# GpSimd adds a constant to VectorE's magnitudes in place of shift matmuls

## The chip, the cores and the metric

The kernel runs on one core of a Trainium2 chip. The metric is device time in microseconds (us) for one launch. All engines of the core are in use: TensorE for matmuls (PE, with PEld for the weight loads that it overlaps), VectorE (DVE), ScalarE (ACT), GpSimd (POOL), and SyncE (SP), which issues all DMAs.

## The reference

Attention over a few inducing points, followed by a rational feed-forward layer. All data are float32.

```python
B, N, m, C = 4, 12480, 32, 128          # x: (4, 12480, 128), inducing: (32, 128)
def mab(q, kv):
    s = (q @ kv.transpose(0, 2, 1)) / sqrt(C)
    a = exp(s - s.max(-1, keepdims=True));  a /= a.sum(-1, keepdims=True) + 1e-9
    return a @ kv
h = mab(I, x)                           # 32 pooled rows per batch
x = mab(x, h).reshape(49920, 128)       # attention of every token to the 32 rows

h = x @ w_in                            # (49920, 2048)
P = a[0] + a[1]*h + a[2]*h**2 + a[3]*h**3
Q = 1 + |b[0]|*|h| + |b[1]|*h**2
out = (P / (Q + 1e-6)) @ w_out          # (49920, 128)
```

The kernel rewrites P/Q. After h is scaled, Q is a constant times (1 + |h|)^2 + c, and P/Q is a linear part, which needs no quotient, plus ((|h| + k1)(h + k2) + k3) times a factor proportional to 1/Q. The constants k1, k2 and k3 come from a and b.

## The kernel before

Work is cut into **units** of 480 tokens by 256 hidden columns. Eight units make a **block**, which is 480 finished output columns; there are 26 blocks per batch and 104 blocks, so 832 units. The attention weights and the pooled rows are folded into TensorE's operands: `st` holds the pooled rows times w_in, `at` the softmax weights, and a unit's h is `at` times `st`.

`fast_ticks` (L787) writes the program one **tick** per unit, even and odd units in turn, as an order that the scheduler keeps on each engine (`keep_in_program_order`). A tick takes a step of several units, which are at different ages. The steps, with a letter each, as they are spoken of from here on:

- **first** (L734): two matmuls of 480 columns, `hp<-at,st`. They write h to a PSUM room `hp`; there are three rooms of two banks.
- **M**, even units: VectorE takes the magnitude, `u<-hp`, by masking the sign bit, and writes half of a pair tile `u`. Odd units get |h| from ScalarE's Abs (`u<-hp,all`) into the other half. For odd units the constant k2 already stands in `st`, and Abs takes it off again with its bias.
- **S**, even units only (`add_shift`, L749): two matmuls `hp<-ones_rows,k_rows` add k2 to h in PSUM, once M has read it.
- **N** (`numerator`, L837): VectorE's `l<-u,all,hp`, (|h| + k1) times (h + k2), into one of twelve rooms `l`. When N has read h, its `hp` room is free.
- ScalarE runs Ln and, four ticks later, Sigmoid on the whole pair (`u<-u` and `u<-u,all`); u then holds the factor proportional to 1/Q. Four pairs get Ln in a row, then four Sigmoid, with a table load at each switch.
- **K**, even units, eleven ticks after M: VectorE's `l<-l,all,u`, (l + k3) times u.
- **T** and **X**, odd units (`last_on_pool`, L842): GpSimd's `u<-l,all` adds k3, writing over the even unit's u, which K must have read; then `l<-u` multiplies.
- **second** (L754), twelve ticks after first: TensorE multiplies the unit with w_out, `po<-l,w_out`, four passes, and so frees its `l` room. The eighth unit of a block adds the linear part (`po<-at,st`); then VectorE copies the block (`oT<-po`) and a DMA writes it out.

Between these steps `side` (L685) places the attention's own work, piece by piece, from two generators: `ahead` (scores and pooled rows of the next batch, its weights) and `attend` (softmax of tokens to the pooled rows). A piece is put into a tick when its estimated cost fits what the tick has to spare on VectorE, GpSimd or TensorE. ScalarE's copies of this work (`hl<-pa`, `eT<-pt`, `gt<-pgt`) are queued by `act` (L220) and written in the next tick by `run_act` (L227). Blocks of x come in by SyncE's queue: `x_rows` and the columns of kind a from six rooms `xa`, five ahead, the columns of kind b from five rooms `xTb`, four ahead. `spread` (L622) copies the weights from `hl` into the operand layout `at` with eight DMAs at a time.

Of the kernel before, what the change touches and what calls it, by code (L numbers as in the profile page):

```python
# [9 lines left out]
F32 = mybir.dt.float32  # L10
# [34 lines left out]
class Params:  # L45
# [46 lines left out]
    def derive(self):  # L92
# [28 lines left out]
        self.n += 2  # L121
        self.k2_parts = self.all[:, self.n - 2:self.n]
        part = self.pool.tile([P, 1], F32R, name="k2_part")
        self.nc.vector.tensor_copy(out=part, in_=self.k2)
        self.nc.vector.tensor_copy(out=self.k2_parts[:, 0:1], in_=part.bitcast(F32))
        self.nc.vector.tensor_tensor(out=self.k2_parts[:, 1:2], in0=self.k2, in1=part.bitcast(F32), op=sub)
# [52 lines left out]
class Kernel:  # L179
# [40 lines left out]
    def act(self, do):  # L220

        if self.direct:
            do()
        else:
            self.act_q.append(do)

    def run_act(self, exps=True):  # L227
        for do in self.act_q:
            do()
        self.act_q = []  # L230
        if exps:
# [35 lines left out]
    def weights(self):  # L267

        parts = []
        for f0 in range(0, self.F, BT):  # L270
            c = slice(f0, min(f0 + BT, self.F))
            parts.append((self.w_in_d[:, c], self.w_in[:, c], c.stop - c.start))
        for f0 in range(0, self.NF, 3):
            c = slice(f0, min(f0 + 3, self.NF))
            dst = self.w_out[:, c].rearrange("p f d -> p (f d)")
            parts.append((self.w_out_d[P * c.start:P * c.stop, :].rearrange("(f p) d -> p f d", p=P), dst, C * (c.stop - c.start)))
        for n, (src, dst, width) in enumerate(parts):
            tag, bufs = ("l", 12) if width > 2 * P else ("oT", 2)
# [58 lines left out]
    def pass1(self, b):  # L337
# [21 lines left out]
        self.xs[b] = [self.x_rows(b, n) for n in range(5)]  # L359
# [46 lines left out]
    def pooled(self, b, own=None):  # L406
# [6 lines left out]
        def turned(g):  # L413
# [7 lines left out]
            self.act(lambda: nc.scalar.activation(eT[:, :, rows], pt[0:TP, :, rows], AF.Identity, bias=0.0, scale=1.0))  # L421
# [8 lines left out]
        for g in range(self.NG):  # L430
# [4 lines left out]
            yield "wait", 0  # L435
            self.free()
            yield from self.landed("x", b, g)
            for k in range(HB * nb):
# [4 lines left out]
                if c == 0 and 4 * g + j + 5 < self.NB:  # L443
                    xs.append(self.x_rows(b, 4 * g + j + 5))
# [70 lines left out]
    def linear(self, b):  # L515
# [8 lines left out]
        self.act(lambda: nc.scalar.activation(gt, pt[:, 0:self.NF], AF.Identity, bias=self.params.lin_shift, scale=self.params.lin_scale))  # L524
        yield "wait", 0
# [70 lines left out]
    def quotients(self, b, r, nb, a):  # L596
# [10 lines left out]
        while self.spreads >= 2:  # L607
# [7 lines left out]
        self.act(lambda: nc.scalar.activation(hl[rows, 0], pt[rows, 0:BT], AF.Identity, bias=0.0, scale=1.0))  # L615
        yield "wait", 0
# [5 lines left out]
    def spread(self, b, r, nb, hl):  # L622
# [12 lines left out]
        self.spreads -= 1  # L635
        yield 0, 0, 0
# [150 lines left out]
    def fast_ticks(self, units):  # L787
# [4 lines left out]
        V, A, p = self.nc.vector, self.nc.scalar, self.params  # L792
# [3 lines left out]
        for t in range(n + 13):  # L796
            u, last, d = at(t), at(t - 1), at(t - 11)
            group, turn = divmod(t - 6, 8)
            w = at(8 * group + 2 * (turn % 4))
            if t % 2:  # L800
                if last:
                    self.add_shift(last)
                if at(t + 1):
                    self.first(at(t + 1))
# [3 lines left out]
                if at(t - 12):  # L808
                    self.second(at(t - 12))
# [3 lines left out]
                self.numerator(last)  # L813
            else:
                early = at(t - 12) and at(t - 12).key[2] > 0
                if early:
                    self.second(at(t - 12))
                else:
                    self.fetched = self.fetch()
                if at(t + 1):  # L820
                    self.first(at(t + 1))
# [15 lines left out]
    def numerator(self, u):  # L837
        if u:
            u.g = self.new(u, "l", 12)
            self.nc.vector.scalar_tensor_tensor(out=u.g, in0=u.u, scalar=self.params.k1, in1=u.h, op0=ALU.add, op1=ALU.mult)  # L840
# [32 lines left out]
    def before(self):  # L873
# [17 lines left out]
        col = self.cp.tile([P, 1], F32, name="k2_col")  # L891
        nc.vector.tensor_tensor(out=self.params.k2_parts, in0=self.params.k2_parts, in1=self.ident[:, 0:2], op=ALU.mult)
        nc.vector.tensor_reduce(out=col, in_=self.params.k2_parts, axis=mybir.AxisListType.X, op=ALU.add)
        self.ones_rows = self.cp.tile([2, BT], F32R, name="ones_rows")
        ones = self.cp.tile([2, 1], F32, name="one")
        nc.vector.memset(ones, 1.0)
        nc.vector.tensor_copy(out=self.ones_rows, in_=ones.broadcast_to((2, BT)))
        self.k2_rows = self.cp.tile([2, P], F32R, name="k2_rows")
        nc.vector.tensor_scalar(out=self.k2_rows, in0=ones.broadcast_to((2, P)), scalar1=col[0:2], scalar2=None, op0=ALU.mult)
# [5 lines left out]
    def main(self, fast):  # L905
# [6 lines left out]
        self.splits, self.spreads, self.scored, self.fetched = 0, 0, -1, False  # L912
# [60 lines left out]
```

## Time and profile before

| | us |
|---|---|
| median of 3 runs (lowest to highest) | 2725.65 (2723.05 to 2727.47) |
| profiled execution, its own time | 2723.84 |
| its span | 2722.0 |

| engine | busy us | share of the span |
|---|---|---|
| PE | 2522.6 | 93% |
| ACT | 2258.3 | 83% |
| DVE | 2133.3 | 78% |
| POOL | 1442.2 | 53% |

The profile's names for tiles are those of the code without numbers. `x832` is a count of instructions. In the chain of waits each step is followed back to what released it, so its sum is the span. A window's answer gives each engine's busy time between two moments. The moment at which a block's output DMA is issued serves as the border of blocks: the first is at 157.56 us, the last at 2717.50.

### The profile page before, as it was taken

What the parts mean: (1) busy time and instruction counts of PE and PEld (TensorE: products, weight loads), DVE (VectorE), ACT (ScalarE), POOL (GpSimd) and SP (SyncE); (2) the same over time, 40 slices, a digit from 0 to 9 for tenths busy, and PEclk for the clock granted to TensorE, in tenths of its full rate; (3) what the DMA queues carried; (4) which work ended last, traced back from release to release, by engine and by line L of the source; (5) the groups of instructions that cost most, each with busy time, mean ns of one, the idle gap of its engine ahead of it and who ended that gap; (6) DMA issues with size and microseconds to landing.
All of it is one profiled execution on the core that took longest, in us unless ns stands there. A gap on an engine that the chain in (4) does not pass through costs nothing.

```text
span 2722.0 us, 25250 instructions
## 1 busy us (share of the span) xinstructions
PE 2522.6 (93%) x8340; PEld 1343.6 (49%) x8340; DVE 2133.3 (78%) x2326; ACT 2258.3 (83%) x1591; POOL 1442.2 (53%) x1004
## 2 busy tenths in 40 slices
PE   7899989999998899999989999998999999899998
PEld 5545445555454455554545555444545445444443
DVE  6478877787878777877887778888888888888886
ACT  1478888888878987878898788898898988899996
POOL 2144555455545555555554555565555555655556
PEclk9699999999999999999999999999999999999999
DMA  9222112112221112022202210001101000000000
GB/s 255 76 76 77 37 33 58 51 55 66 76 58 44 30 39 73 19 76 87 64 16 73 62 29 28 21 18 55 48 26 41 29 22 22 26 19 26 19 19 16
DMA packets 117365, 133.77 MB, mean 49 GB/s; under 512 B 13544, under 2 KB 115816, under 8 KB 117224
## 3 DMA queue, kind: packets, MB, share of 16 engines
q1 hardware_dynamic: 117224, 132.06, 17.1%
q8 instruction: 68, 1.11, 0.2%
q14 instruction: 73, 0.60, 0.1%
HBM read 80.89 MB, written 25.56 MB: 39 GB/s over the span
## 4 chain that ended last, share of the span: by engine, by line
PE 63%; DVE 21%; ACT 7%; issue 3%; SPq 2%; DMA 2%; POOL 1%; DVEq 0%; ACTq 0%; POOLq 0%
PE po L163 32%; PE hp L163 20%; DVE l L163 11%; DVE u L163 9%; ACT u L163 5%; PE pd L163 3%; PE ph L163 3%; SPq L163 2%; PE pc L163 2%; ACT L163 1%; POOL l L163 1%; DMA raw<-w_in 1%; PE pl L163 1%; DVE oT L163 1%; PE pgt L163 1%
## 5 line engine op out<-in xcount | busy, mean ns | idle before, releaser
L163 PE MATMUL po<-l,w_out 128*128 128x480 f32 x3328 | 1482.0, 579 | 18.7 <-DVE oT L163 14.4
L163 DVE SCALAR_TENSOR_TENSOR l<-u,all,hp 128x960 f32<-128x960 f32 x832 | 1006.5, 1210 | 377.0 <-PE po L163 211.0
L163 POOL TENSOR_SCALAR u<-l,all 128x960 f32<-128x960 f32 x416 | 444.5, 1069 | 1105.1 <-DVE l L163 894.4
L163 POOL TENSOR_TENSOR l<-u 128x960 f32<-128x960 f32 x416 | 930.1, 2236 | 34.7
L163 PEld LDWEIGHTS po<-l,w_out 128*128 128x128 f32 x3328 | 627.1, 192 | 555.3 <-issue 447.2
L163 ACT ACTIVATE u<-u,all 128x1920 f32<-128x1920 f32 x416 | 776.0, 1889 | 1.2
L163 ACT ACTIVATE u<-u 128x1920 f32<-128x1920 f32 x416 | 737.3, 1797 | 1.1
L163 PE MATMUL hp<-at,st 128*128 128x480 f32 x1664 | 672.0, 485 | 33.6 <-DVE l L163 31.8
L163 ACT ACTIVATE u<-hp,all 128x960 f32<-128x960 f32 x416 | 438.1, 1053 | 288.8 <-PE hp L163 281.3
L163 DVE SCALAR_TENSOR_TENSOR l<-l,all,u 128x960 f32<-128x960 f32 x416 | 511.6, 1230 | 90.8 <-ACT u L163 90.6
L163 DVE TENSOR_SCALAR u<-hp 128x960 int32<-128x960 int32 x416 | 478.7, 1151 | 3.1 <-PE hp L163 3.1
L163 PEld LDWEIGHTS hp<-at,st 128*128 128x128 f32 x1664 | 280.8, 191 | 340.7 <-issue 270.9
L163 PE MATMUL hp<-ones_rows,k_rows 2*128 2x480 f32 x832 | 293.3, 431 | 114.1 <-DVE u L163 112.9
L163 ACT ACT_TABLE_LOAD x235 | 301.5, 1283 | 4.8 <-PEq L966 0.7
L163 PEld LDWEIGHTS hp<-ones_rows,k_rows 2*128 2x128 f32 x832 | 123.0, 185 | 309.1 <-DVE u L163 258.0
L163 DVE COPY oT<-po 128x480 f32<-128x480 f32 x104 | 68.2, 656 | 70.8 <-PE po L163 70.7
L163 PEld LDWEIGHTS pd<-HT,xTb 128*120 128x120 f32 x832 | 103.3, 198 | 13.8 <-issue 10.0
L163 PE MATMUL ph<-x,eT 120*32 120x129 f32 x832 | 104.9, 277 | 3.8 <-DMA x<-x_t 2.6
L163 PEld LDWEIGHTS ph<-x,eT 120*32 120x32 f32 x832 | 87.3, 111 | 31.6 <-issue 18.1
L163 PE MATMUL pd<-HT,xTb 128*120 128x32 f32 x832 | 99.7, 276 | 0.8 <-DVE hl L163 0.4
L163 PE MATMUL po<-at,st 128*128 128x480 f32 x104 | 79.6, 765 | 0.0
L163 PE MATMUL pc<-xTa,ind 128*128 128x480 f32 x156 | 69.9, 566 | 0.0
(92 smaller groups left out, 586.1 us busy)
## 6 DMA issues: line engine op xcount, KB each, us to landing
x<-x_t SPq DMA_DIRECT2D x104, 240.0 KB, 3.7
xTb<-x_c SPq DMA_DIRECT2D x104, 240.0 KB, 2.9
at<-hl SPq DMA_DIRECT2D x416, 60.0 KB, 2.0
out<-oT SPq DMA_DIRECT2D x104, 240.0 KB, 2.0
xTa<-x_c SPq DMA_DIRECT2D x78, 240.0 KB, 3.0
xTw<-x_c SPq DMA_DIRECT2D x5, 960.0 KB, 11.7
raw<-w_in SPq DMA_DIRECT2D x4, 480.0 KB, 15.0
raw<-w_out SPq DMA_DIRECT2D x5, 384.0 KB, 6.1
```

The source lines that it names most:

```text
L163: ins = call(*args, **kw)
```

## The change

1. S is gone, with the two-row operands `ones_rows` and `k2_rows` and the instructions that prepare them. In its place GpSimd adds k1 to M's result in the even tick, `l<-u,all` (**G**, a TENSOR_SCALAR of 128 x 960), and the even unit's N becomes (h + k2) times that: its tensor inputs are h in PSUM and l in SBUF, and it no longer reads u. The odd unit's N is as it was.
2. In an even tick M comes ahead of the odd unit's N on VectorE, and TensorE has first in another place of the tick.
3. There are fourteen rooms `l` in place of twelve. The even unit takes its room a tick earlier, at G.
4. ScalarE's queued copies are written one tick later than before, and the generator that queued one waits until it is written. The transposes `pa` also wait until two ticks have passed since the spread before the last was done.
5. `xa` has four rooms in place of six, `xTb` four in place of five; rows and columns of x are fetched three or four blocks ahead.

```diff
     def act(self, do):
+        done = []
         if self.direct:
             do()
         else:
-            self.act_q.append(do)
+            self.act_q.append((self.tick, do, done))
+            while not done:
+                yield "wait", 0
     def run_act(self, exps=True):
-        for do in self.act_q:
+        while self.act_q and self.act_q[0][0] < self.tick:
+            _, do, done = self.act_q.pop(0)
             do()
-        self.act_q = []
+            done.append(1)
...
     def x_rows(self, b, n):
-        t = self.ap.tile([TP, HB, C + 1], F32, tag="xa", name=f"x{b}_{n}", bufs=6)
+        t = self.ap.tile([TP, HB, C + 1], F32, tag="xa", name=f"x{b}_{n}", bufs=4)
...
-            t = self.ap.tile([C, BT], F32, tag="xTb", name=f"xTb{b}_{n}", bufs=5)
+            t = self.ap.tile([C, BT], F32, tag="xTb", name=f"xTb{b}_{n}", bufs=4)
...
-                if c == 0 and 4 * g + j + 5 < self.NB:
-                    xs.append(self.x_rows(b, 4 * g + j + 5))
+                if c == 0 and 0 < 4 * g + j < self.NB - 3:
+                    xs.append(self.x_rows(b, 4 * g + j + 3))
...
-        while self.spreads >= 2:
+        while self.spreads >= 2 or self.tick < self.sent[0] + 2 and not self.boot:
             yield "wait", 0
...
-    def add_shift(self, u):
-        for k in range(2):
-            self.nc.tensor.matmul(u.h[:, k], self.k2_rows, self.ones_rows, start=False, stop=True, skip_group_check=True)
...
+            late = at(t - 12) and at(t - 12).key[2] == 0
+            if late:
+                self.fetched = self.fetch()
+            if t % 2 and at(t + 1):
+                self.first(at(t + 1))
+            if at(t - 12) and not late:
+                self.second(at(t - 12))
+            if t % 2 == 0 and at(t + 1):
+                self.first(at(t + 1))
             if t % 2:
-                if last:
-                    self.add_shift(last)
-                if at(t + 1):
-                    self.first(at(t + 1))
                 if u:
                     u.u = last.pair[:, 1]
                     A.activation(u.u, u.h, AF.Abs, bias=p.back, scale=1.0)
-                if at(t - 12):
-                    self.second(at(t - 12))
                 if d:
                     V.scalar_tensor_tensor(out=d.g, in0=d.g, scalar=p.k3, in1=d.u, op0=ALU.add, op1=ALU.mult)
                     self.last_on_pool(at(t - 10), d)
-                self.numerator(last)
+                if last:
+                    V.scalar_tensor_tensor(out=last.g, in0=last.h, scalar=p.k2, in1=last.g, op0=ALU.add, op1=ALU.mult)
             else:
-                ...
-                self.numerator(last)
                 if u:
                     u.pair = self.mp.tile([P, 2, 2, BT], F32, tag="u", name=f"u{u.i}", bufs=7)
                     u.u = u.pair[:, 0]
                     V.tensor_scalar(out=u.u.bitcast(I32), in0=u.h.bitcast(I32), scalar1=0x7FFFFFFF, scalar2=None, op0=ALU.bitwise_and)
+                if last:
+                    last.g = self.new(last, "l", 14)
+                    V.scalar_tensor_tensor(out=last.g, in0=last.u, scalar=p.k1, in1=last.h, op0=ALU.add, op1=ALU.mult)
+                if u:
+                    u.g = self.new(u, "l", 14)
+                    G.tensor_scalar(out=u.g, in0=u.u, scalar1=1.0, scalar2=p.k1, op0=ALU.mult, op1=ALU.add)
...
-            if t % 2 == 0 and not early and at(t - 12):
+            if late:
                 self.second(at(t - 12))
```

How this moves the instructions is seen best in the last batch, where little attention work stands between the units. The names are batch, block and unit of the block (hp3_20_4 is unit 4 of block 20 of batch 3) and a running number. First TensorE around that unit, before:

```order
L163 MATMUL hp3_20_3_13539<-at3_5_0_13244,st_3_8873 128x480 x2
L163 MATMUL hp3_20_2_13525<-ones_rows_548,k2_rows_552 128x480 x2
L163 MATMUL hp3_20_4_13549<-at3_5_0_13244,st_3_8873 128x480 x2
L163 MATMUL po3_18_0_13472<-l3_18_7_13408,w_out_90 128x480 x2
L163 MATMUL po3_18_0_13472<-at3_4_1_13025,st_3_8873 128x480
```

and in the change:

```order
L157 MATMUL hp3_20_3_13133<-at3_5_0_12849,st_3_9162 128x480 x2
L157 MATMUL hp3_20_4_13143<-at3_5_0_12849,st_3_9162 128x480 x2
L157 MATMUL po3_18_0_13071<-l3_18_7_13009,w_out_90 128x480 x2
L157 MATMUL po3_18_0_13071<-at3_4_1_12638,st_3_9162 128x480
L157 MATMUL hp3_20_5_13158<-at3_5_0_12849,st_3_9162 128x480 x2
```

The shift of unit 2 is gone from between the firsts of units 3 and 4, which now stand back to back. VectorE over the same ticks, before:

```order
L163 SCALAR_TENSOR_TENSOR l3_20_3_13568<-u3_20_2_13544,all_196,hp3_20_3_13539 128x960
L163 TENSOR_SCALAR u3_20_4_13570<-hp3_20_4_13549 128x960
L163 SCALAR_TENSOR_TENSOR l3_19_2_13449<-l3_19_2_13449,all_196,u3_19_2_13434 128x960
L163 SCALAR_TENSOR_TENSOR l3_20_4_13587<-u3_20_4_13570,all_196,hp3_20_4_13549 128x960
L163 SCALAR_TENSOR_TENSOR l3_20_5_13595<-u3_20_4_13570,all_196,hp3_20_5_13565 128x960
```

and in the change:

```order
L157 TENSOR_SCALAR u3_20_4_13161<-hp3_20_4_13143 128x960
L157 SCALAR_TENSOR_TENSOR l3_20_3_13163<-u3_20_2_13136,all_193,hp3_20_3_13133 128x960
L157 SCALAR_TENSOR_TENSOR l3_19_2_13034<-l3_19_2_13034,all_193,u3_19_2_13030 128x960
L157 SCALAR_TENSOR_TENSOR l3_20_4_13165<-hp3_20_4_13143,all_193,l3_20_4_13165 128x960
L157 TENSOR_SCALAR u3_20_6_13187<-hp3_20_6_13171 128x960
```

The order was N, M, K, N and is M, N, K, N; the second N of a pair (unit 4) reads h and l where it read u and h. GpSimd, before:

```order
L163 TENSOR_SCALAR u3_19_0_13410<-l3_19_1_13432,all_196 128x960
L163 TENSOR_TENSOR l3_19_1_13432<-u3_19_0_13410 128x960
L163 TENSOR_SCALAR u3_19_2_13434<-l3_19_3_13467,all_196 128x960
L163 TENSOR_TENSOR l3_19_3_13467<-u3_19_2_13434 128x960
L163 TENSOR_SCALAR u3_19_4_13469<-l3_19_5_13494,all_196 128x960
```

and in the change:

```order
L157 TENSOR_SCALAR u3_19_0_13007<-l3_19_1_13032,all_193 128x960
L157 TENSOR_TENSOR l3_19_1_13032<-u3_19_0_13007 128x960
L157 TENSOR_SCALAR l3_20_4_13165<-u3_20_4_13161,all_193 128x960
L157 TENSOR_SCALAR u3_19_2_13030<-l3_19_3_13066,all_193 128x960
L157 TENSOR_TENSOR l3_19_3_13066<-u3_19_2_13030 128x960
```

G of unit 4 of block 20 stands between X of block 19's unit 1 and T of its unit 3. T of unit 3 waits for K of block 19's unit 2, whose u it writes over.

More of the change, by code (lines that the diff above doesn't have):

```diff
@@ L120, in derive @@
         self.back = self.ts(self.k2, -1.0, mult)
[L121 to L126, printed above, removed]
         top = self.mul(self.mul(self.mul(a3, alpha), self.mul(alpha, alpha)), self.recip(gamma))
@@ L277, in weights @@
         for n, (src, dst, width) in enumerate(parts):
-            tag, bufs = ("l", 12) if width > 2 * P else ("oT", 2)
+            tag, bufs = ("l", 14) if width > 2 * P else ("oT", 2)
             raw = self.mp.tile([P, width], mybir.dt.int64, tag=tag, name=f"raw{n}", bufs=bufs)
@@ L306, in columns @@
     def columns(self, b, kind):
-        depth = 5 if kind == "a" else 4
-        ts = [self.x_columns(b, n, kind) for n in range(depth)]
+        ts = [self.x_columns(b, n, kind) for n in range(4)]
         def turns():
             for n in range(self.NB):
-                if n + depth < self.NB:
-                    ts.append(self.x_columns(b, n + depth, kind))
                 yield ts.pop(0)
+                if n + 4 < self.NB:
+                    ts.append(self.x_columns(b, n + 4, kind))
         return turns()
@@ L358, in pass1 @@
             self.free()
-        self.xs[b] = [self.x_rows(b, n) for n in range(5)]
+        self.xs[b] = [self.x_rows(b, n) for n in range(4)]
         yield "v", 0.1
@@ L420, in turned @@
             eT = ap.tile([TP, HB, P], F32, tag="eT", name=f"eT{b}_{g}", bufs=2)
-            self.act(lambda: nc.scalar.activation(eT[:, :, rows], pt[0:TP, :, rows], AF.Identity, bias=0.0, scale=1.0))
+            yield from self.act(lambda: nc.scalar.activation(eT[:, :, rows], pt[0:TP, :, rows], AF.Identity, bias=0.0, scale=1.0))
             eTs.append(eT)
@@ L523, in linear @@
         gt = ap.tile([P, 512], F32, tag="gs", name=f"gt{b}", bufs=2)[:, 0:self.NF * M].rearrange("p (f m) -> p f m", m=M)
-        self.act(lambda: nc.scalar.activation(gt, pt[:, 0:self.NF], AF.Identity, bias=self.params.lin_shift, scale=self.params.lin_scale))
-        yield "wait", 0
+        yield from self.act(lambda: nc.scalar.activation(gt, pt[:, 0:self.NF], AF.Identity, bias=self.params.lin_shift, scale=self.params.lin_scale))
         self.free()
@@ L614, in quotients @@
         hl = ap.tile([P, 2, BT], F32R, tag="hl", name=f"hl{b}_{r}", bufs=2)
-        self.act(lambda: nc.scalar.activation(hl[rows, 0], pt[rows, 0:BT], AF.Identity, bias=0.0, scale=1.0))
-        yield "wait", 0
+        yield from self.act(lambda: nc.scalar.activation(hl[rows, 0], pt[rows, 0:BT], AF.Identity, bias=0.0, scale=1.0))
         yield "v", 0.65
@@ L635, in spread @@
         self.spreads -= 1
+        self.sent = self.sent[1], self.tick
         yield 0, 0, 0
@@ L812, in fast_ticks @@
                     self.last_on_pool(at(t - 10), d)
-                self.numerator(last)
-            else:
[L815 to L821, printed above, removed]
-                self.numerator(last)
+                if last:
+                    V.scalar_tensor_tensor(out=last.g, in0=last.h, scalar=p.k2, in1=last.g, op0=ALU.add, op1=ALU.mult)
+            else:
                 if u:
@@ L832, in fast_ticks @@
             self.side(u or units[-1])
-            if t % 2 == 0 and not early and at(t - 12):
+            if late:
                 self.second(at(t - 12))
         self.fetch()
[L837 to L840, printed above, removed]
     def last_on_pool(self, d, before):
@@ L852, in general_ticks @@
             self.first(u)
-            d, y, g, h = self.new(u, "u", 7), self.new(u, "l", 12), self.new(u, "l", 12), u.h
+            d, y, g, h = self.new(u, "u", 7), self.new(u, "l", 14), self.new(u, "l", 14), u.h
             r = self.ps_h.tile([P, 2, 512], F32, tag="hp", name=f"r{u.i}")[:, :, 0:BT]
@@ L890, in before @@
         self.params.derive()
[L891 to L899, printed above, removed]
         self.ceps = self.cp.tile([P, 1], F32, name="ceps")
```

7 lines of the change are left out of this document (3 added, 4 removed).

## The prediction

> **What bounds the kernel now.** I first cut the span into stretches with the windows view, at the moments where output blocks are issued, and counted the copies `oT<-po` in each. The columns are length, then busy time and count of PE, PEld, DVE, ACT and POOL.
>
> ```profile
> 157.56:1746.13 1588.57, 1507.67 (x5200) 815.95 (x5199) 1247.87 (x1321) 1339.09 (x945) 845.78 (x603) 0.99 0.19 53
> 1746.13:2678.96 932.83, 852.53 (x2524) 430.80 (x2524) 772.21 (x728) 841.47 (x579) 535.31 (x329) 0.99 0.10 28
> 2678.96:2722.00 43.04, 32.00 (x74) 13.87 (x74) 20.29 (x16) 21.34 (x14) 25.70 (x15) 0.96 0.06 20
> 2522.41:2544.76 22.35, 20.44 (x57) 10.04 (x57) 18.77 (x18) 20.72 (x15) 13.19 (x9) 1.00 0.03 11
> ...
> 157.56:1746.13 1588.57, 39.98 (x61) 0.99 0.19 53
> 1746.13:2678.96 932.83, 26.27 (x40) 0.99 0.10 28
> ```
>
> Stage A (the first row, 61 blocks) has the attention work of the next batch beside the units. It takes 1588.57 / 61 = 26.04 us a block; per block PE is busy 24.72, ACT 21.95, DVE 20.46, POOL 13.87. Stage B (40 blocks) has only the softmax of its own tokens: 23.32 a block, PE 21.31, ACT 21.04, DVE 19.31, POOL 13.38. The fourth row is one clean block of stage B: 22.35. There no engine is full, not even ACT with 20.72, so a chain must set the time. The chain of waits shows it, one pair of units after the other:
>
> ```profile
> 2544.66 1.20 DVE l L163
> 2545.86 1.08 DVE u L163
> 2546.94 0.04 issue
> 2546.98 1.33 PE hp L163 x4
> 2548.32 1.62 PE po L163 x4
> ...
> 2550.06 1.22 DVE l L163
> ```
>
> N of an odd unit (1.20), then M (1.08), then on TensorE S and the next first (1.33), then a second (1.62), whose `l` room the next N needs: 5.40 us a pair, four pairs and the block's copy make the 22.35. In stage A the attention's matmuls stand in this chain too, and PE's 24.72 of 26.04 is nearly the whole.
>
> **The change part by part.** *S goes.* The timeline of the same pair, and what TensorE waited:
>
> ```profile
> 2546.98 0.70 PE L163 MATMUL hp<-ones_rows,k_rows 2*128 2x480 f32 x2 [0.31 <-DVE u L163]
> 2547.61 0.70 PE L163 MATMUL hp<-at,st 128*128 128x480 f32 x2
> ...
> PE hp L163 <- DVE u L163: 112.9, 237, 1.9
> ```
>
> S holds TensorE 2547.61 - 2546.98 = 0.63 us a pair, 2.5 a block, 262 in all, and makes it wait 112.9 for M. PE falls to 22.2 a block in stage A, 18.8 in B.
>
> *M first, fourteen rooms.* N no longer stands ahead of M, and the room that an N needs was freed by a second two units earlier. The links 1.20 and 1.62 leave the chain. If nothing took its place, a clean block would fall to ACT's 20.7.
>
> *G and the new N.* G is a TENSOR_SCALAR of T's shape:
>
> ```profile
> L163 POOL TENSOR_SCALAR u<-l,all 128x960 f32<-128x960 f32 x416 | 444.5, 1069 | 1105.1 <-DVE l L163 894.4 <-PE hp L163 130.5 <-ACT u L163 30.5
> ```
>
> so 1.07 us each, 4.3 a block: GpSimd's sum rises to 17.5 in a clean block and 18.2 in stage A, far from full. But it does not share freely with K. Here are K's group (mean 1230 ns), one K and what GpSimd did beside it, and the end of the kernel:
>
> ```profile
> L163 DVE SCALAR_TENSOR_TENSOR l<-l,all,u 128x960 f32<-128x960 f32 x416 | 511.6, 1230 | 90.8 <-ACT u L163 90.6
> ...
> 1156.97 2.12 DVE L163 SCALAR_TENSOR_TENSOR l<-l,all,u 128x960 f32<-128x960 f32 x1
> ...
> 1156.82 1.26 POOL L163 TENSOR_TENSOR st<-gs,st 64x512 fp32r<-64x512 f32 x1
> ...
> 2698.54 5.89 DVE L163 SCALAR_TENSOR_TENSOR l<-l,all,u 128x960 f32<-128x960 f32 x3
> ...
> 2701.47 1.96 POOL L163 TENSOR_SCALAR u<-l,all 128x960 f32<-128x960 f32 x1 [1.12 <-PE po L163]
> ...
> 2706.48 1.06 POOL L163 TENSOR_SCALAR u<-l,all 128x960 f32<-128x960 f32 x1
> 2707.63 2.21 POOL L163 TENSOR_TENSOR l<-u 128x960 f32<-128x960 f32 x1
> 2709.82 1.07 POOL L163 TENSOR_SCALAR u<-l,all 128x960 f32<-128x960 f32 x1
> ```
>
> The GpSimd instruction ended at 1158.08, K at 1159.09: K did its work in the 1.01 us after it, not beside it. At the end of the kernel a T took 1.96 in place of 1.06 beside three K in a row. So K and GpSimd take turns, in both directions. Before, this cost almost nothing: T waits for K and X for T, and both are over when the next K comes. Now G stands between X and the next K. One pair then needs, in turn: K after the instruction ahead of it 1.01; from K's end to T's start 0.11; T to X 1.15 (2706.48 to 2707.63); X to the next instruction 2.19 (2707.63 to 2709.82); G 1.07. The 0.11 is from these rows, where K ends at 2548.05:
>
> ```profile
> 2546.84 1.21 DVE L163 SCALAR_TENSOR_TENSOR l<-l,all,u 128x960 f32<-128x960 f32 x1
> 2547.97 1.21 DVE L163 SCALAR_TENSOR_TENSOR l<-u,all,hp 128x960 f32<-128x960 f32 x1
> ...
> 2548.16 1.07 POOL L163 TENSOR_SCALAR u<-l,all 128x960 f32<-128x960 f32 x1 [2.31 <-DVE l L163]
> ```
>
> The sum is 5.53 us. Where K is first and G follows it, the 0.11 is hidden: 5.42. I take 5.5, so 22.0 a block. With K's full 1.21, X's 2.23 and a gap before G like the 0.11 it would be 5.9, my upper end. VectorE's other three instructions, about 3.3 (K to N is 1.13 from start to start), fit beside G, T and X, 4.4. M is ready for G: N and M need 2.2 after K, T and X 3.45. Behind G on its queue stand T and X, and behind G on VectorE the even N, whose `hp` room the next first needs; that N comes after K anyway.
>
> That the new N does not take turns too is read from an instruction with its pattern, one input in PSUM and one in SBUF, of which most ran beside a GpSimd instruction:
>
> ```profile
> L163 DVE TENSOR_TENSOR hl<-pa,hl x28: 640/648/658, 84.7 to 2463.0; 128x480 fp32r<-128x480 f32 x24, 64x480 fp32r<-64x480 f32 x4
> ```
>
> Its longest is 658 ns against a median of 648. So N stays at 1.21; the other end is K's 1.01 on top.
>
> The Trainium skill (page SBUF — State Buffer, section Who interferes with whom) says that a VectorE instruction with two SBUF inputs contends with a GpSimd instruction that reads SBUF, the second to issue being blocked until the first is done, and that one with at most one SBUF input outside the two-port modes does not. By it the sum is the one below, and were the rule not to hold, the first rival's; the trace agrees, with K's 2.12 and the 658 ns.
>
> *Other GpSimd work in stage A* takes its turn too:
>
> ```profile
> L163 POOL TENSOR_TENSOR a<-a,asm 120x512 f32<-120x512 f32 x17 | 17.9, 1051 | 0.0
> L163 POOL TENSOR_TENSOR st<-gs,st 64x512 fp32r<-64x512 f32 x12 | 15.2, 1270 | 1.6 <-DVE st L163 0.9
> L163 POOL MEMSET x<- 120x4 f32 x78 | 6.4, 105 | 29.7 <-PE ph L163 29.3
> ```
>
> The first two rows are 33.1 us, 0.5 a block; I take 0.6 with the few smaller ones, and add 0.4 for hand-overs, an estimate: some 34 instructions over 61 blocks, each behind a VectorE step like the `hl` row's 0.65. The memsets' wait of 29.7 stays hidden while GpSimd is behind TensorE.
>
> *Copies a tick later.* They take away ScalarE waits:
>
> ```profile
> ACT hl L163 <- DMA at<-hl: 44.5, 13, 4.4
> ACT eT L163 <- PE pt L163: 31.0, 15, 5.5
> DVE l L163 <- ACT u L163: 112.0, 98, 4.3
> ```
>
> ACT would not be the last in the forecast, so I count them only in stage B's unevenness. They cost nothing unless the attention work becomes late, and each piece is ready many ticks ahead. If ACT were the bound, they would be worth up to 75 us.
>
> *Fewer rooms for x.* The issues are the same in number, but SyncE's queue works in order, and eight `at` issues stand in it. The second row is the x tiles' time from issue to landing in the main loop:
>
> ```profile
> 2545.20 5.54 SPq L163 DMA_DIRECT2D at<-hl  x8
> ...
> DMA to landing us min/median/max: 2.8/3.4/5.5
> ```
>
> The last block of a group of four is now asked for as the group begins, a tick (26.04 / 8 = 3.3) before TensorE needs it. Normally it is issued as soon as its room is free, which is earlier. Behind a spread it can be 5.5 + 3.4 - 3.3 = 5.6 late. I take 0, since TensorE has 23.0 - 22.2 = 0.8 to spare per block in stage A.
>
> *The sum,* against the profiled execution's 2723.84 (span 2722.0; the median is 1.8 above it). Stage A: the largest sum becomes the turns, 22.0 + 0.6 + 0.4 = 23.0. Today a block is 1.3 above its largest sum (26.04 - 24.72); I keep that: 24.3, so -1.74 x 61 = -106. Stage B: clean blocks 22.0. Today the mean is 0.97 above the clean block; ScalarE's waits for `at<-hl` are part of it, so I keep 0.7: 22.7, so -0.62 x 40 = -25. Ahead of 157.56 and behind 2678.96 I change nothing. 2723.84 - 131 + 1.8 = 2595. My own range for this case, turns of 5.4 to 5.75 with the same margins, is 2560 to 2690.
>
> **The rivals.** The second of them rests on Sigmoid's group:
>
> ```profile
> L163 ACT ACTIVATE u<-u,all 128x1920 f32<-128x1920 f32 x416 | 776.0, 1889 | 1.2
> ```
>
>  *The turns are slack.* K and G miss each other, or G slips into VectorE's waits, and the engines' sums decide: stage A 22.2 + 1.3 = 23.5, stage B 20.7 + 0.7 = 21.4, so 2723.84 - 155 - 77 + 1.8 = 2494. For it: in stage A PE and ACT are only 1 us below the turns. Against: in a clean block K comes at a fixed place, and nothing keeps G away from it.
>
> *Slower: K late behind ScalarE.* The first K after four Ln waits for a table load and a Sigmoid; 112.0 us over 104 blocks, 1.1 each, are lost so today. T, X and G stand behind K, and with turns that nearly fill the block nothing makes up for it. If this adds the length of one Sigmoid (1.89) to each of 101 blocks, the time is 2595 + 191 = 2786; it decides from 131 / 101 = 1.3 a block. Against: ACT's 20.7 leaves it 1.3 a clean block.
>
> *Slower: late x.* 28 groups of softmax scores (seven a batch) and 21 of pooled rows, each 5.6 late: 274, so 2869; it decides from 2.7 each. *Slower: the new N takes turns too:* 1.01 more a pair, 4 a block, 404 over 101 blocks, so about 3000; the 658 ns speak against it. *No change:* turns at the upper end, 5.85, take back 1.3 a block, and the 131 is gone.
>
> **How the numbers follow.** Forecast 0.60; slack turns 0.20; no change 0.05; K late 0.08, x late 0.04, N in turns 0.03. What differs by less than 0.2%, about 5 us, cannot be told from no change. Faster is 0.60 + 0.20 = 0.80, same 0.05, slower 0.15. The range takes in the first rival and the upper part of the turns: 2490 to 2700, leaving out the slower cases and little else.
>
> **What would show it.** Right: K's mean well above 1.23, with many at 1.6 to 2.3 us beside a GpSimd instruction; the clean block near 22.0, its chain running over K, T, X and G (POOL a large share); PE without `<-DVE u`; N at 1.21. The first rival: K at 1.21, clean blocks at 21, ACT near full. The second: `DVE l <- ACT u` beyond 200 us. The third: `PE <- DMA x` or `xTb`, today almost nil, in tens of us. The forecast is wrong if clean blocks fall below 21.3 or stand above 23.

## The result, and the profile after

| | before | the change |
|---|---|---|
| median (lowest to highest), us | 2724.35 (2719.74 to 2727.47) | 2600.66 (2599.82 to 2603.05) |
| profiled span, us | 2722.0 | 2598.0 |
| stage A, us a block (61 blocks) | 26.04 | 24.50 |
| stage B, us a block (40 blocks) | 23.32 | 22.66 |
| a clean block of stage B, us | 22.35 | 21.69 |

The ratio of the times is 0.9549, 95% interval 0.9532 to 0.9565. The span is 124.0 us shorter: 94.1 in stage A, 26.3 in stage B, 3.8 ahead of the first output block (157.56 before, 153.80 now), and the tail is 0.1 longer. (The stretch ahead of the first block varies from 145.6 to 159.7 us over the runs of this document, so its 3.8 is not read as an effect.) The three stretches by the windows view of the change (length, then busy time and count of PE, PEld, DVE, ACT and POOL, the granted clock, the DMA share, GB/s):

```profile
153.80:1648.24 1494.44, 1336.90 (x4643) 751.65 (x4641) 1278.05 (x1311) 1332.02 (x943) 1170.83 (x842) 0.97 0.20 56
1648.24:2554.82 906.58, 755.37 (x2274) 390.31 (x2272) 794.93 (x738) 845.32 (x580) 805.12 (x494) 0.99 0.10 29
2424.67:2446.36 21.69, 17.84 (x51) 8.81 (x49) 18.95 (x18) 20.87 (x15) 20.26 (x13) 1.00 0.13 35
```

Per block of stage A, PE is now busy 21.9, ACT 21.8, DVE 21.0, POOL 19.2. In the clean block no engine is full, as before, so again a chain sets it. The shares of the chain of waits on the page, by engine before, then by engine and by line in the change:

```profile
PE 63%; DVE 21%; ACT 7%; issue 3%; SPq 2%; DMA 2%; POOL 1%; DVEq 0%; ACTq 0%; POOLq 0%
...
PE 36%; DVE 24%; POOL 16%; ACT 13%; issue 6%; DMA 1%; SPq 1%; DVEq 0%; ACTq 0%; POOLq 0%
PE po L157 21%; DVE l L157 14%; POOL l L157 12%; ACT u L157 10%; PE hp L157 7%; DVE u L157 5%; POOL u L157 3%; PE ph L157 3%; ACT L157 3%; PE pd L157 3%; DVE oT L157 2%; SPq L157 1%; PE pc L157 1%; POOL a L157 1%; DVE asm L157 1%
```

TensorE's share has fallen by 27 points, and GpSimd's has risen by 15. Now the groups of the four steps that the prediction speaks of. In order: first, K, G, and the new N.

```profile
L157 PE MATMUL hp<-at,st 128*128 128x480 f32 x1664 | 660.8, 486 | 289.7 <-DVE l L157 254.0
L157 DVE SCALAR_TENSOR_TENSOR l<-l,all,u 128x960 f32<-128x960 f32 x416 | 574.6, 1382 | 122.0 <-ACT u L157 121.4
L157 POOL TENSOR_SCALAR l<-u,all 128x960 f32<-128x960 f32 x416 | 599.3, 1441 | 56.6 <-DVE u L157 53.2
L157 DVE SCALAR_TENSOR_TENSOR l<-hp,all,l 128x960 f32<-128x960 f32 x416 | 504.0, 1211 | 165.6 <-POOL l L157 157.0
```

The wait of first for M is gone; what it waits for now is an N that has still to free its `hp` room, 254.0 us in all. K's mean rose from 1230 to 1382 ns, G's is 1441 where T, an instruction of the same kind and shape, takes 1067, and N stands at 1211. The tile view gives least, median and longest in ns:

```profile
L157 DVE SCALAR_TENSOR_TENSOR l<-l,all,u x416: 1124/1253/2756, 120.2 to 2578.3; 128x960 f32<-128x960 f32 x139
L157 POOL TENSOR_SCALAR l<-u,all x416: 1055/1073/2237, 91.1 to 2561.9; 128x960 f32<-128x960 f32 x139
L157 DVE SCALAR_TENSOR_TENSOR l<-hp,all,l x416: 1198/1211/1221, 93.3 to 2563.9; 128x960 f32<-128x960 f32 x139
```

K and G have long tails; the new N has none, though 412 of its 416 instructions overlap a GpSimd instruction that is no memset. Both are held back, K beyond 1.3 us in 153 of its 416 instructions and G in 162; the other K stay near their plain length. The clean block, from its timeline, shows the turns (start, length):

```profile
2426.18 1.07 POOL L157 TENSOR_SCALAR l<-u,all 128x960 f32<-128x960 f32 x1
...
2426.75 1.50 DVE L157 SCALAR_TENSOR_TENSOR l<-l,all,u 128x960 f32<-128x960 f32 x1
...
2428.35 1.07 POOL L157 TENSOR_SCALAR u<-l,all 128x960 f32<-128x960 f32 x1 [1.10 <-DVE l L157]
...
2429.50 2.24 POOL L157 TENSOR_TENSOR l<-u 128x960 f32<-128x960 f32 x1
...
2431.49 1.26 DVE L157 SCALAR_TENSOR_TENSOR l<-l,all,u 128x960 f32<-128x960 f32 x1
...
2431.73 1.96 POOL L157 TENSOR_SCALAR l<-u,all 128x960 f32<-128x960 f32 x1
...
2433.67 1.07 POOL L157 TENSOR_SCALAR u<-l,all 128x960 f32<-128x960 f32 x1
2433.73 1.22 DVE L157 SCALAR_TENSOR_TENSOR l<-hp,all,l 128x960 f32<-128x960 f32 x1 [0.97 <-POOL l L157]
...
2439.09 1.06 POOL L157 TENSOR_SCALAR u<-l,all 128x960 f32<-128x960 f32 x1
...
2444.51 1.06 POOL L157 TENSOR_SCALAR u<-l,all 128x960 f32<-128x960 f32 x1
```

In the first pair G is ahead: it ends at 2427.25, K 1.00 later at 2428.25, and T waits for K. In the second pair T and X run to 2431.74. K was issued at 2431.49, 0.25 before X's end, and ends 1.01 after it. G was issued beside K and ends at 2433.69, 0.94 after K's end at 2432.75. The next T follows at once, 5.32 after the last; the even N waits 0.97 for G. The two pairs after it, also with K ahead of G, take 5.42 each from T to T, the prediction's figure for that order; the T after those comes at 2450.05, 5.54 later, and there G is ahead again, for which the prediction had 5.53. The four make 21.70, the clean block.

### The profile page after: what moved, and what is told of

The parts are those of the page before. It is cut to its first block, busy times and chain, and to the rows that moved or that the text cites. A ratio compares the mean times of both kernels' runs of the same rounds, so it can differ in the third digit from the quotient of the medians.

```text
span 2598.0 us, 24003 instructions
## 1 busy us (share of the span) xinstructions
PE 2243.7 (86%) x7508; PEld 1234.1 (48%) x7508; DVE 2185.6 (84%) x2318; ACT 2254.7 (87%) x1590; POOL 2053.0 (79%) x1420
## 4 chain that ended last, share of the span: by engine, by line
PE 36%; DVE 24%; POOL 16%; ACT 13%; issue 6%; DMA 1%; SPq 1%; DVEq 0%; ACTq 0%; POOLq 0%
PE po L157 21%; DVE l L157 14%; POOL l L157 12%; ACT u L157 10%; PE hp L157 7%; DVE u L157 5%; POOL u L157 3%; PE ph L157 3%; ACT L157 3%; PE pd L157 3%; DVE oT L157 2%; SPq L157 1%; PE pc L157 1%; POOL a L157 1%; DVE asm L157 1%
## 5 line engine op out<-in xcount | busy, mean ns | idle before, releaser
L157 PE MATMUL hp<-at,st 128*128 128x480 f32 x1664 | 660.8, 486 | 289.7 <-DVE l L157 254.0
L157 POOL TENSOR_SCALAR u<-l,all 128x960 f32<-128x960 f32 x416 | 443.8, 1067 | 366.7 <-DVE l L157 353.3
L157 DVE SCALAR_TENSOR_TENSOR l<-l,all,u 128x960 f32<-128x960 f32 x416 | 574.6, 1382 | 122.0 <-ACT u L157 121.4
L157 POOL TENSOR_SCALAR l<-u,all 128x960 f32<-128x960 f32 x416 | 599.3, 1441 | 56.6 <-DVE u L157 53.2
L157 DVE SCALAR_TENSOR_TENSOR l<-hp,all,l 128x960 f32<-128x960 f32 x416 | 504.0, 1211 | 165.6 <-POOL l L157 157.0
L157 PEld LDWEIGHTS hp<-at,st 128*128 128x128 f32 x1664 | 289.4, 194 | 626.6 <-issue 434.1
L157 DVE SCALAR_TENSOR_TENSOR l<-u,all,hp 128x960 f32<-128x960 f32 x416 | 500.1, 1202 | 0.0
L157 PEld LDWEIGHTS ph<-x,eT 120*32 120x32 f32 x832 | 87.6, 111 | 32.5 <-issue 23.5
```

The lines of the kernel that those rows point to most:

```text
L157: ins = call(*args, **kw)
```

## The experiments

Stage figures below are us a block, by the same 61 and 40 blocks as above. They are from one profiled execution of each run. The differences that matter are between runs and the change's 2600.7. The rows after the change were measured in three groups of four; the kernel before, measured with each group, had medians between 2719 and 2724, so a difference of some 5 us between groups is not read. Letters are the steps' names.

| run | median us | ratio to before, 95% | stage A | stage B | clean |
|---|---|---|---|---|---|
| the change | 2600.7 | 0.9549 (0.9532 to 0.9565) | 24.50 | 22.66 | 21.69 |
| K with one tensor input in SBUF | 2531.9 | 0.9302 (0.9271 to 0.9333) | 24.14 | 21.57 | 20.57 |
| no G | 2526.5 | 0.9283 (0.9252 to 0.9314) | 24.03 | 21.54 | 20.56 |
| G only writes | 2530.1 | 0.9300 (0.9267 to 0.9332) | 24.09 | 21.64 | 20.57 |
| G twice | 2933.1 | 1.0776 (1.0740 to 1.0813) | 27.22 | 26.76 | 26.10 |
| S kept, no G | 2639.2 | 0.9696 (0.9659 to 0.9733) | 25.47 | 22.01 | 20.72 |
| copies in the next tick | 2663.3 | 0.9782 (0.9748 to 0.9817) | 25.40 | 22.88 | 21.70 |
| twelve rooms | 2647.0 | 0.9716 (0.9683 to 0.9750) | 24.86 | 23.30 | 22.21 |
| S for half the even units | 2603.5 | 0.9554 (0.9520 to 0.9587) | 24.81 | 22.14 | 20.65 |
| twelve rooms, x rooms as before | 2634.9 | 0.9679 (0.9659 to 0.9699) | 24.69 | 23.30 | 22.19 |
| the same, copies in the next tick | 2649.8 | 0.9732 (0.9712 to 0.9752) | 24.99 | 23.18 | 22.19 |
| S for half, in stage B alone | 2572.9 | 0.9450 (0.9432 to 0.9468) | 24.49 | 21.99 | 20.63 |
| S for all, in stage B alone | 2572.5 | 0.9441 (0.9426 to 0.9457) | 24.53 | 21.97 | 20.70 |

### Do the turns of K and GpSimd set the clean block?

The theory is the prediction's: K and any GpSimd instruction that reads SBUF take turns, and the ring of K, T, X and G is the clean block. The rival is its first one: the turns are slack, and the sums of the engines decide. Four runs tell these apart: K without its second SBUF tensor, no G at all, G that writes but does not read, and G twice.

K with one tensor input in SBUF; the other input is a PSUM tile, and the product with u is left out:

```diff
-V.scalar_tensor_tensor(out=d.g, in0=d.g, scalar=p.k3, in1=d.u, op0=ALU.add, op1=ALU.mult)
+V.scalar_tensor_tensor(out=d.g, in0=d.g, scalar=d.u[:, 0, 0:1], in1=last.h if last else units[-1].h, op0=ALU.add, op1=ALU.mult)
```

> The change with K reading one SBUF tensor: its second input is the h of the unit just before it in PSUM, its scalar a column of u (so it still waits for u, and T still waits for it). The product with u in K is left out, so the even units' results are wrong. Theory of turns (K and GpSimd's reading instructions exclude each other because K has two SBUF inputs): K's mean falls from 1.38 to 1.21 us, G's from 1.44 to 1.07, clean blocks from 21.7 to ScalarE's 20.9, the whole to about 2510 us. Rival (the pair's time comes from GpSimd's queue or from VectorE's order, whatever K reads): about 2600, K and G as they were.

No G; the even N multiplies by u, so k1 is left out:

```diff
-V.scalar_tensor_tensor(out=last.g, in0=last.h, scalar=p.k2, in1=last.g, op0=ALU.add, op1=ALU.mult)
+V.scalar_tensor_tensor(out=last.g, in0=last.h, scalar=p.k2, in1=last.u, op0=ALU.add, op1=ALU.mult)
...
-G.tensor_scalar(out=u.g, in0=u.u, scalar1=1.0, scalar2=p.k1, op0=ALU.mult, op1=ALU.add)
```

> The change with G left out and nothing in its place: the even unit's N is (h + k2) times u, so k1 is left out for the even units. Turns: only T and X are left beside K, and they are over before the next K; K at 1.21, clean blocks at 20.9, stage A 0.5 to 1 a block shorter, about 2500 us in all. Rival (ScalarE, or the shallower fetching of x, already sets the time): within 10 us of 2600.

G as an instruction that writes its tile and reads nothing:

```diff
-G.tensor_scalar(out=u.g, in0=u.u, scalar1=1.0, scalar2=p.k1, op0=ALU.mult, op1=ALU.add)
+G.memset(u.g, 1.0)
```

> The change with G as a memset of the same 128 x 960 tile to 1.0, so |h| + k1 is left out for the even units: a GpSimd instruction at the same place that N waits for, which writes SBUF and does not read it. If only reads exclude K: K at 1.21 beside it, about 2510 us. If any GpSimd instruction excludes K: K stays near 1.38, and the time at 2600 less four times what the memset is shorter than 1.07 in each of 101 blocks. This is the row that tells reads from writes.

G written twice, so that its second run repeats the first:

```diff
 G.tensor_scalar(out=u.g, in0=u.u, scalar1=1.0, scalar2=p.k1, op0=ALU.mult, op1=ALU.add)
+G.tensor_scalar(out=u.g, in0=u.u, scalar1=1.0, scalar2=p.k1, op0=ALU.mult, op1=ALU.add)
```

> The change with G issued twice (the second writes the same values again). Turns: one more reading instruction in each pair's ring, 5.42 + 1.1 = 6.5 us a pair, clean blocks 26 us, about 3000 us in all. Rival (sums of busy time: GpSimd's 17.5 in a clean block becomes 21.8, just above ScalarE's 20.9): clean blocks 22 to 22.5, 2620 to 2650 us.

The three runs in which K and G no longer take turns land within 6 us of each other, 2526.5 to 2531.9, and all their clean blocks are 20.56 or 20.57. They miss the 2500 to 2510 that was expected by 20 to 27 us, since stage A gains 0.36 to 0.47 a block and not 0.5 to 1. Their durations by tile, first K with one SBUF tensor and G beside it:

```profile
L157 POOL TENSOR_SCALAR l<-u,all x416: 1058/1072/1231, 92.5 to 2494.7; 128x960 f32<-128x960 f32 x139
L157 DVE SCALAR_TENSOR_TENSOR l<-l,u,hp x416: 1121/1208/1217, 119.0 to 2510.0; 128x960 f32<-128x960 f32 x139
```

Then K as it is, and the G that only writes:

```profile
L157 DVE SCALAR_TENSOR_TENSOR l<-l,all,u x416: 1124/1217/2905, 116.9 to 2508.5; 128x960 f32<-128x960 f32 x139
L157 POOL MEMSET l<- x416: 888/901/925, 89.9 to 2492.1; 128x960 f32 x139
```

In the first the tails are gone on both sides: 1217 and 1231 ns are the longest. In the second GpSimd still has a third instruction in the pair, and it never waits, 925 ns at most, though 244 of the 416 overlap a K, as in this clean block:

```profile
2425.41 0.91 POOL L157 MEMSET l<- 128x960 f32 x1
...
2425.77 1.21 DVE L157 SCALAR_TENSOR_TENSOR l<-l,all,u 128x960 f32<-128x960 f32 x1
```

The two overlap for 0.55 us, and both have their plain length. What long K there are (up to 2905) stand beside T or X or the attention's GpSimd work, which still read. So GpSimd's being busy costs nothing; its reading of SBUF beside K does. The Trainium skill (page SBUF — State Buffer, section Who interferes with whom) says just this, that a VectorE instruction with two inputs in SBUF contends with a GpSimd instruction that reads SBUF and not with one that only writes; the 925 ns agree.

With G twice the ring should grow by one G, 1.07, and 5.42 + 1.07 = 6.49. The clean block is 26.10, a pair 6.53. The windows row of that block and two groups of that run:

```profile
2832.66:2858.76 26.10, 19.64 (x51) 9.47 (x49) 18.96 (x18) 21.06 (x14) 25.38 (x17) 0.94 0.03 10
```

```profile
L157 POOL TENSOR_SCALAR l<-u,all 128x960 f32<-128x960 f32 x832 | 1209.0, 1453 | 97.2 <-DVE u L157 55.1 <-PE pg L157 0.5 <-PE pd L157 0.5
...
L157 DVE SCALAR_TENSOR_TENSOR l<-hp,all,l 128x960 f32<-128x960 f32 x416 | 506.0, 1216 | 559.8 <-POOL l L157 532.2 <-POOL x L157 27.6
```

POOL is busy 25.38 of 26.10, the even N waits 532.2 us for G (157.0 in the change), and the time is 332 us over the change's (some 400 were expected). The busy sums alone would have given 22 to 22.5. The ring sets the clean block. It does not set stage A as firmly. This is the run without G:

```profile
154.44:1620.53 1466.09, 1337.09 (x4643) 757.01 (x4641) 1233.48 (x1311) 1328.35 (x943) 851.30 (x599) 0.96 0.20 57
...
2440.99:2461.55 20.56, 17.84 (x51) 8.79 (x49) 18.63 (x18) 20.50 (x15) 13.24 (x9) 1.00 0.03 12
```

Its clean block is ScalarE's: 20.50 of 20.56. But stage A falls only from 24.50 to 24.03. So G with its turns costs the change 1.1 a block in stage B and 0.47 in stage A: 45 + 29 = 74 us, which is the difference of the medians, 2600.7 - 2526.5. By the run in which no turns at all are left (K with one SBUF tensor) it is 69.

What sets stage A then? I took the largest engine sum of each of its 61 blocks by itself, and the mean of these: 25.05 before, 23.09 in the change, 22.86 without G. Before, this is 0.3 above PE's own mean of 24.72, since PE was the largest in 50 of the 61 blocks. Now it is in 29, ACT in 22, DVE in 9, POOL in one. Two blocks of the change's stage A:

```profile
177.60:206.94 29.34, 25.10 (x93) 14.84 (x91) 20.60 (x23) 22.33 (x16) 20.49 (x14) 0.94 0.36 101
899.34:922.13 22.79, 18.27 (x55) 9.30 (x53) 19.20 (x18) 22.63 (x17) 19.26 (x13) 1.00 0.03 11
```

The first holds much attention work for TensorE (25.10), the second is ScalarE's (22.63 of 22.79). A block takes at least its own largest sum, so with these borders the mean of the largest, not the largest mean, is the floor: 23.09, of which the distance to PE's 21.9 is 1.2. (Time in which an instruction is held back counts as busy here.) The rest to 24.50, 1.4, is time in which no engine is full, where in the run without G it is 24.03 - 22.86 = 1.2. What makes up these 1.2 was not tested.

### Which part of the change gained what?

S kept, and no G: parts 2 to 5 of the change alone. The edit is shown shortened; it also prepares the operands of S again.

```diff
+if t % 2 and last:
+    self.add_shift(last)    # two matmuls, as before; the ones are one column, broadcast
 if t % 2 and at(t + 1):
     self.first(at(t + 1))
...
-V.scalar_tensor_tensor(out=last.g, in0=last.h, scalar=p.k2, in1=last.g, op0=ALU.add, op1=ALU.mult)
+V.scalar_tensor_tensor(out=last.g, in0=last.u, scalar=p.k1, in1=last.h, op0=ALU.add, op1=ALU.mult)
...
-G.tensor_scalar(out=u.g, in0=u.u, scalar1=1.0, scalar2=p.k1, op0=ALU.mult, op1=ALU.add)
```

> Parts 2 to 5 of the change without part 1: S stays (its row of ones is a column read 480 times), G is not issued, the even N is as before. As forecast: S is 2.5 us of TensorE a block, which binds only in stage A; there blocks of about 25.4 (24.5 in the change), while in clean blocks, with no turns left, ScalarE's 20.6 decides and not the change's 21.7; about 2610 us. Rival (the shift is the gain): clean blocks near 22.4, about 2690 us.

It takes 2639.2, 85 below before. So most of the gain, 85 of 124, needs no G. The expected 2610 was too low: stage A, 25.47, is as foreseen, and stage B has its clean block of 20.72 but a mean of 22.01. The windows of its stages:

```profile
156.39:1710.27 1553.88, 1486.87 (x5133) 811.44 (x5131) 1238.24 (x1311) 1334.32 (x943) 850.30 (x599) 0.98 0.19 54
1710.27:2590.61 880.34, 848.08 (x2593) 435.59 (x2592) 775.24 (x738) 838.65 (x580) 544.28 (x333) 0.99 0.10 30
```

In stage A PE is busy 24.4 of 25.47: TensorE is the bound, and G's replacing of S is worth 0.97 a block there. In stage B it costs 0.65 a block: 22.01 with S, 22.66 with G. G pays where TensorE is the bound and costs where GpSimd's ring is, and the net is 61 x 0.97 - 40 x 0.65 = 33. The two profiled executions differ by 33.8, the medians by 38.5.

S for the even units 0 and 4 of a block, G for 2 and 6, throughout (here and below, the lines that bring S back are left out):

```diff
+def by_shift(self, u):
+    b, n, q = u.key
+    return q in (0, 4)
```

> The change with S in place of G for half of the even units (units 0 and 4 of a block), the rest as in the change. Turns: two of four pairs have no G, so a clean block needs 2 x 5.42 + 2 x 4.4 = 19.7 on that ring and ScalarE's 20.6 decides, 1.1 shorter; in stage A TensorE gains 1.25 us and the ring loses 2: between 24.2 and 24.8 a block. 2545 to 2590 us in all. Rival (each edit adds what it saves elsewhere): 2600 or more.

2603.5 against 2600.7: no difference that can be told, where 2545 to 2590 was expected; but not for want of an effect. Stage A is 0.31 a block worse and stage B 0.52 better, and 61 x 0.31 and 40 x 0.52 cancel.

Twelve rooms (the other places with the number change with it):

```diff
-last.g = self.new(last, "l", 14)
+last.g = self.new(last, "l", 12)
...
-u.g = self.new(u, "l", 14)
+u.g = self.new(u, "l", 12)
```

> The change with twelve rooms l in place of fourteen. G then waits for the second of the same tick. As forecast (the rooms took the link of second to N out of the chain): the link comes back through G, clean blocks above 21.7 by 0.3 to 1, 2620 to 2690 us. Rival (the turns alone set the pair, 5.42): unchanged within 10 us.

46 us slower, clean block 22.21. What comes back is the wait for a second to free a room, now on G:

```profile
L157 POOL TENSOR_SCALAR l<-u,all 128x960 f32<-128x960 f32 x416 | 607.3, 1460 | 201.9 <-PE po L157 160.9 <-DVE u L157 29.3 <-DVE l L157 5.4
```

In the change G's whole idle time ahead of it is 56.6. The link from second to room was real, and the two rooms take it away.

### The copies a tick later, and the rooms for x

ScalarE's copies in the next tick, as before, and all else as in the change:

```diff
-while self.act_q and self.act_q[0][0] < self.tick:
+while self.act_q:
```

> The change with part 4 undone for the copies: ScalarE's queued copies are written in the next tick again (the wait of the transposes for the spread stays). As forecast: ScalarE is not last in the change, so within 10 us of 2600; its waits for the transposes come back, some 30 us off the path. Rival (stage A's blocks are set by ScalarE's order): 0.5 a block or more in stage A, 2630 or above.

63 us slower, where at most 10 was expected: 0.90 a block in stage A, 0.22 in stage B. Two kinds of wait come with it; the last two rows are the change's:

```profile
ACT hl L157 <- DMA at<-hl: 39.5, 12, 3.9
PE pd L157 <- DMA xTb<-x_c: 29.1, 8, 8.1
PE ph L157 <- DMA x<-x_t: 10.3, 6, 8.0
...
PE pd L157 <- DMA xTb<-x_c: 3.1, 2, 1.9
PE ph L157 <- DMA x<-x_t: 5.2, 5, 2.4
```

ScalarE's wait of the first row isn't there in the change. The longest wait for x, in the timeline:

```profile
336.40 0.37 SPq L157 DMA_DIRECT2D out<-oT  x1
...
336.88 4.96 SPq L157 DMA_DIRECT2D at<-hl  x8
...
341.88 1.54 SPq L157 DMA_DIRECT2D xTb<-x_c  x3
...
344.83 1.81 PE L157 MATMUL pd<-HT,xTb 128*120 128x32 f32 x8 [8.07 <-DMA xTb<-x_c]
```

TensorE is ready at 336.76. SyncE's queue then holds an output block and a spread's eight DMAs; x is issued behind all nine, at 341.88, lands some 3 us later, and TensorE has waited 8.07. This is the prediction's rival of late x: 8 waits for `xTb` and 6 for `x` in this run.

To part the two kinds of wait, the x rooms were set back to six and five, with x fetched as far ahead as before the change. That has room only beside twelve l rooms. First with the copies late:

```diff
-t = self.ap.tile([TP, HB, C + 1], F32, tag="xa", name=f"x{b}_{n}", bufs=4)
+t = self.ap.tile([TP, HB, C + 1], F32, tag="xa", name=f"x{b}_{n}", bufs=6)
...
-    t = self.ap.tile([C, BT], F32, tag="xTb", name=f"xTb{b}_{n}", bufs=4)
+    t = self.ap.tile([C, BT], F32, tag="xTb", name=f"xTb{b}_{n}", bufs=5)
...
-if c == 0 and 0 < 4 * g + j < self.NB - 3:
-    xs.append(self.x_rows(b, 4 * g + j + 3))
+if c == 0 and 4 * g + j + 5 < self.NB:
+    xs.append(self.x_rows(b, 4 * g + j + 5))
```

> The change with twelve rooms l and the earlier handling of x back: six rooms xa, five xTb, fetched five and four blocks ahead. Against the run with twelve rooms alone (2647 us). My reading that the fewer x rooms of the change cost nothing: 2642 to 2652. Rival, x is late at times and the waits are hidden in others' names: 2620 to 2640.

2634.9, where twelve rooms alone took 2647.0. By these medians the fewer x rooms cost 12 us there, against the expectation of nothing and as the rival had it. The two are from different groups and the intervals of their ratios just overlap, so the size is uncertain; the traces bear it out, since TensorE's waits for x of all kinds fall from 12.0 us to 2.8. Then with the copies in the next tick as well:

```diff
-while self.act_q and self.act_q[0][0] < self.tick:
+while self.act_q:
```

> As the run before (twelve rooms l, the earlier x rooms), and ScalarE's copies written in the next tick again. With the fewer x rooms this edit cost 63 us, and TensorE's waits for x rose with it. If it costs by late x: within 15 us of the run before, and no waits of TensorE for x. If it costs by what ScalarE waits for in its own queue (the weights' spread, the transposes): 45 to 65 us above the run before, with those ScalarE waits as in the earlier run.

2649.8, 15 above the run before, the size foreseen for late x as the cause, and TensorE's waits for `xTb` are gone from the view of waits, while ScalarE's stay:

```profile
ACT hl L157 <- DMA at<-hl: 31.3, 8, 4.6
```

So the delay of the copies is worth 15 us with many x rooms and 63 with few. The difference, 48, goes with late x, of which the traces show 33 directly: TensorE's waits for x of all kinds rise by 34.5 us with few rooms (9.8 to 44.3) and by 1.1 with many (2.8 to 3.9). That the 15 are ScalarE's waits and what follows them is likely, not shown. One doubt stays: the two pairs of runs differ in the l rooms too, and with twelve the clean block is longer, which may hide a part of either.

### A version from what was learned

G belongs in stage A and S in stage B. Two versions use G for all even units before block 62, counted from 0, and from there on S, for two of four even units or for all:

```diff
+def by_shift(self, u):
+    b, n, q = u.key
+    return b * self.NB + n >= 62 and q in (0, 4)
```

> The change, but from block 62 on (where no attention work of a next batch is left) the even units 0 and 4 of a block get k2 by the shift matmuls S instead of G; ahead of that G serves all even units. If what a stage costs hangs only on its own form: stage A as in the change, 24.49 us a block, and stage B as with half the units shifted, 22.12: 2600.7 - 40 x (22.67 - 22.12) = 2579 us. If the gain of the shifts in stage B is only a delay that is made up elsewhere: 2601, no difference.

```diff
-    return b * self.NB + n >= 62 and q in (0, 4)
+    return b * self.NB + n >= 62
```

> As the run before, but from block 62 on all even units get k2 by S, and G ends there. Stage A as in the change, 24.49 us a block, stage B as with S kept throughout, 22.00: 2600.7 - 40 x (22.67 - 22.00) = 2574 us. If TensorE, with 21.2 of 22.0 a block busy then, sets stage B's unevenness: above the run before, 2580 to 2590.

2572.9 and 2572.5, where 2579 and 2574 were expected: 28 us below the change, and intervals of the ratio clear of the change's (0.9432 to 0.9468 and 0.9426 to 0.9457 against 0.9532 to 0.9565). Both beat both kernels. The stages of the first:

```profile
152.84:1647.03 1494.19, 1338.49 (x4649) 751.96 (x4647) 1280.27 (x1311) 1332.14 (x943) 1164.54 (x839) 0.97 0.20 56
1647.03:2526.56 879.53, 800.45 (x2433) 414.61 (x2432) 789.83 (x738) 838.28 (x580) 659.15 (x414) 0.99 0.10 30
```

Stage A is the change's to 0.01, and stage B the one of the run with S throughout. ACT is now at 20.96 of 21.99 a block in stage B, and PE at 20.0. With S for all PE is at 21.2, a little above ACT's 20.97, and the loss that the expectation named for that case, 2580 to 2590, didn't show: half and all come out the same, so S costs little there even then.

## Why the prediction was right, and where it was not

The time, 2600.7, is 6 us above the 2595 forecast.

- **S goes:** right. PE fell to 21.9 and 18.9 a block (22.2 and 18.8 foreseen), and no wait of TensorE for M is left.
- **The turns:** right in mechanism and size. Four runs bear it out in both directions. 5.5 was taken; the pairs of a clean block take 5.32 to 5.54, 5.42 on average. The terms are less exact than the sum: with K ahead, K takes 1.01 or its full 1.21, and G ends 0.85 to 0.94 after it in the block shown, where 1.01 and 1.07 were added.
- **The new N** doesn't take turns: right, 1221 ns at the longest.
- **M first, fourteen rooms:** right that the room's link leaves the chain (twelve rooms cost 46 us), but its weight was not seen: parts 2 to 5 without G bring 85 of the 124 us.
- **Stage B:** 22.66 against 22.7 from clean blocks of 21.69 (22.0 foreseen) and unevenness of 0.97 (0.7 foreseen). Two misses of 0.3 cancel. The unevenness did not shrink at all: it was 0.97 before too.
- **Stage A:** 24.50 against 24.3, by a sum whose terms are wrong. It was to be turns, 23.0, and the old unevenness of 1.3. So this hit is luck in part. The step that failed is "the largest sum becomes the turns": stage A takes 24.03 without G, and 24.14 with no turns left at all. By the sums it is PE and ACT, at 21.9 and 21.8 on average, in blocks that differ: 1.0 for the mean of the largest sums over PE's mean (22.86 to 21.9), 1.2 for idle time inside the blocks, and 0.47 for G and its turns. That TensorE binds there the run with S shows (0.97 a block); ScalarE's part is read from the sums alone. The same error stands in the first rival: its 23.5 for stage A kept the 1.3 as well, and with G's turns gone stage A is 24.03 to 24.14 and the whole 2526.5 to 2531.9, not 2494.
- **Copies a tick later:** the worst mis-sized term. It was counted at about nothing because ScalarE would not be last. Undone, it costs 63 us. The step overlooked that this part is what makes part 5 bearable: by the four runs some 48 of the 63 go with late x.
- **Fewer rooms for x:** taken at 0; about 12 us, beside twelve l rooms, where it could be measured. Late x was put at 5.6 for each spread in the way; the longest seen was 8.07. The rival had the right place and mechanism, but the change, by its later copies, holds it to 3.1 and 5.2 us in all.
- **K late behind ScalarE:** not so, `DVE l <- ACT u` is 121.4 against 112.0 before. It does rise to 231 to 246 us in the three runs without turns of K and G, where ScalarE is the bound, and they are faster all the same.

## What to carry to other kernels

Cost an instruction that is moved to an idle engine by what it shares with its neighbours, and by stage: here the same step won 0.97 us a block where TensorE was the bound and lost 0.65 where the ring of GpSimd and VectorE was, and using each form in its own stage was worth 28 us more. When the largest engine comes down to the level of the next ones, the distance from block time to the largest sum grows; add up the largest sum of each block, not the sums of the stage. An edit that only delays work can carry another one that shortens a queue's lead, so cost the two together.

## What was not expected of the hardware

- How sharply the exclusion goes by reads: the GpSimd instruction that only writes stayed within 888 to 925 ns in all 416 cases, 244 of them beside a K, where the reading G, 1055 ns at the least, went up to 2237.
- The granted clock was lower where TensorE had less to do: 0.94 in the clean block with G twice, at 19.64 busy of 26.10, against 1.00 in the change's at 17.84 of 21.69. The mean hides two levels, as rows of that run at the block's start show:

```profile
2828.90:2832.31 3.41, 1.50 (x5) 0.52 (x5) 1.46 (x2) 3.08 (x2) 3.23 (x4) 1.00 0.00 0
2832.31:2835.73 3.42, 3.42 (x7) 1.85 (x7) 3.42 (x4) 2.38 (x2) 3.32 (x3) 0.50 0.20 72
2835.73:2858.76 23.03, 16.57 (x46) 7.90 (x45) 15.89 (x16) 18.68 (x13) 22.41 (x15) 1.00 0.00 0
```

The clock was 0.50 for 3.4 us and 1.00 for the rest of the block, and in the 3.41 us ahead TensorE was busy for 1.50. That the light load caused it, and what it cost, was not tested.
